# Clustered attention with transposed q and k, full float32 products and a new instruction order

## The chip, the cores and the metric

One core of a Trainium2 chip runs the whole program: TensorE (PE in the profile), VectorE (DVE), ScalarE (ACT), GpSimd (POOL) and SyncE (SP, which issues DMAs). The metric is the device time of one execution in microseconds. The kernel before takes 862.75 us, the median of three runs (862.23 to 864.58).

## What is computed

Sixteen attention heads (2 batches of 8, 768 tokens, 64 dimensions) in which a query sees only the keys of its own cluster, then a gated feed-forward layer, then a mixture of eight experts. The change lies in the attention part:

```python
q_assign = np.argmax(np.einsum('bhsd,hcd->bhsc', q_n, c_n), axis=-1)   # 16 centroids per head
k_assign = np.argmax(np.einsum('bhsd,hcd->bhsc', k_n, c_n), axis=-1)
mask = q_assign[:, :, :, None] == k_assign[:, :, None, :]
scores = np.where(mask, q @ k.T / 8, -1e9)                             # per head, 768 x 768
attn = softmax(scores)
x = attn @ v
x = _moe_ref(x, w_gate, w_val, w_out)       # sigmoid(x w_gate) * (x w_val) @ w_out
out = _moe2_ref(x, ...)                     # every token to one of 8 experts, 192 places each
```

## The kernel before, in words

**Stages.** Attention over 16 heads, 0 to 286 us; the feed-forward layer `Moe1`; its second product, the routing of tokens and the experts (`Gemm`, `Routing`, `Moe2`). `Moe1` follows attention in program order; the instructions of the rest are laid out by due times (`Streams`).

**Attention.** The class `Attention` has one method per step, and each step runs once (or once per tile) in each head. `run` sorts all steps of all heads by `ORDER[step] + n * PERIOD`, n being the head, and issues them in that sequence. Every engine works through its own instructions strictly in this order (`manual_schedule`), so `ORDER` is a hand-laid software pipeline: its keys are model times in us, and only the resulting sequence on each engine counts.

**Steps of a head.** `LD` (L109) loads q, k and v (192 KB each) with tokens on partitions. Products are made of float32r operands, each split into a part rounded to float32r and the remainder (`hi`, `lo`, L116 and L119): `Q8`, `QH`, `QL`, `KH`, `KL`, `K2`, `VH`, `VL` do so for q, k and v, mostly on GpSimd. `T_` (L157) transposes the halves of q and k on TensorE, 24 pieces of 128 columns per head (twelve for `T2`, twelve for `T1`), and `Y_` copies them from PSUM with ScalarE. `D_` (L173) multiplies them with the centroids, two times six matmuls of 256 columns; `DA`, `DD` add the two precision halves; `G1` to `G7` (L194) find the best centroid and write a one-hot code of 16 columns next to q and k, which `T1` transposes along with the low halves. `S_` (L214) makes a tile of 128 x 768 scores with four matmuls, two of which carry the code as 16 more rows, so that keys of other clusters get a huge negative score. `M_` takes the row maximum on VectorE, `E_` the exponential and row sum on ScalarE, `A_` and `C_` the reciprocal, `N_` scales P on GpSimd. `PT` (L253) transposes P in four pieces of 128 x 128 per PSUM bank, 36 pieces per head. `HI` (ScalarE, L263) and `LO` (VectorE, L267) split each transposed bank, and `AV` (L270) multiplies both with v: four matmuls of 256 columns per bank, 36 per head, the two halves of v side by side in the 128 output partitions. `OC` and `OA` add the output halves, `XH` and `XL` split the result for `Moe1`.

**PSUM.** Eight banks: three named `t` in turn (T, D, PT and others), two buffers of two banks for S, one for `av`.

**Weights.** The feed-forward weights come as float64 bits and are converted by `from64` (L369 to L384, one ScalarE and six VectorE steps). `weights(0)` and `weights(1)` convert the first two blocks of 128 columns; they are placed by a scheduler among the instructions of attention, `weights(1)` not ahead of the instructions in `LATE_W1` (L345).

## Time and profile before

| | us |
|---|---|
| median of three runs | 862.75 |
| profiled execution, its own time | 862.27 |
| its span, first to last instruction | 860.5 |
| attention, first S to last AV | 20.4 to 286.5 |
| from there to the end | 574.0 |

The profile is of one execution. A busy share counts the time in which an engine works on at least one instruction; TensorE's matmuls overlap, so their printed durations add up to more than their time, and the distance between starts is used where their pace is wanted. PE is the matmul, PEld the weight load that runs beside it. "L276" is line 276 of the kernel. The granted clock of TensorE has two levels, 1.2 and 2.4 GHz, printed as a share of the higher one.

### The profile page before, as it was taken

How to read it: one execution, taken by the hardware profiler on the slowest of the kernel's cores; microseconds unless marked ns; L12 is line 12 of the kernel's file. 1: busy time of each engine (PE TensorE's matmuls, PEld its weight loads, DVE VectorE, ACT ScalarE, POOL GpSimd, SP SyncE). 2: the span in 40 equal slices, each digit the busy share in tenths (PEclk: the TensorE clock that was granted, in tenths of full speed). 3: DMA queues.
4: the chain of work that ended last, by engine and by line, in shares of the span. 5: the costliest groups of instructions: out<-in, count | busy, mean ns of one | idle time of the engine just before them, and what ended most of it. 6: DMA issues, size and time to landing. Idle time of an engine off the chain costs nothing. (4 is left out here: it accounts for less than half of the span.)

```text
span 860.5 us, 15425 instructions
## 1 busy us (share of the span) xinstructions
PE 812.6 (94%) x5321; PEld 687.6 (80%) x5321; DVE 692.1 (80%) x1835; ACT 468.7 (54%) x993; POOL 245.7 (29%) x339
## 2 busy tenths in 40 slices
PE   3899999999999899999999999999999889889997
PEld 3799999999999687777777777887878676767886
DVE  6899999999996989998872205889988688988992
ACT  4799998998987433333321212234343534454882
POOL 4687788888865000000000000000020210211211
PEclk8999999999999999999999999999999888798999
DMA  5201101101000144453430503143261444445961
GB/s 158 81 29 37 48 29 51 35 29 56 2 1 1 57 166 145 147 185 133 141 105 1 195 1 135 50 136 102 96 208 26 123 151 131 134 143 169 309 239 37
DMA packets 51518, 86.52 MB, mean 101 GB/s; under 512 B 5592, under 2 KB 24048, under 8 KB 51440
## 3 DMA queue, kind: packets, MB, share of 16 engines
q1 hardware_dynamic: 47760, 75.53, 27.0%
q0 software_dynamic: 2048, 6.29, 2.4%
q10 hardware_dynamic: 1632, 3.72, 1.2%
q8 instruction: 42, 0.69, 0.3%
q14 instruction: 36, 0.29, 0.1%
HBM read 72.93 MB, written 12.60 MB: 99 GB/s over the span
## 5 line engine op out<-in xcount | busy, mean ns | idle before, releaser
L1095 ACT ACTIVATE w2h<-raw 128x512 fp32r<-128x512 f32 x128 | 78.8, 632 | 60.3 <-DMA raw<-in_moe_w 59.6
L267 DVE TENSOR_TENSOR ptl<-t,pth 128x512 fp32r<-128x512 f32 x144 | 94.4, 683 | 11.9 <-ACT pth L263 11.7
L229 DVE TENSOR_REDUCE sm<-s 128x1 f32<-128x768 f32 x96 | 91.2, 950 | 9.5 <-PE s L220 9.0
L117 POOL TENSOR_SCALAR P<-P,sm 128x768 f32<-128x768 f32 x96 | 86.6, 910 | 26.5 <-DVE sm L247 15.9
L657 PE MATMUL acc<-wos,yhh 128*128 128x512 f32 x288 | 91.8, 400 | 0.0
L220 PE MATMUL s<-tr 128*128 128x512 f32 (+3 forms) x384 | 90.0, 356 | 1.4 <-ACT P L234 1.2
L263 ACT ACTIVATE pth<-t 128x512 fp32r<-128x512 f32 x144 | 80.9, 600 | 14.8 <-PE t L259 12.6
L234 ACT ACTIVATE P<-s,sm 128x768 f32<-128x768 f32 x96 | 87.0, 906 | 2.1 <-DVE sm L229 2.1
L1098 DVE TENSOR_TENSOR w2l<-raw,w2h 128x512 fp32r<-128x512 f32 x128 | 84.4, 682 | 0.6 <-ACT w2h L1095 0.5
L259 PE MATMUL t<-idf,P 128*128 128x128 f32 x576 | 78.9, 273 | 0.4 <-DVE ptl L267 0.4
L1185 PE MATMUL acc<-xt,w2l 128*128 128x256 f32 x256 | 68.3, 305 | 6.8 <-DVE w2l L1098 6.8
L259 PEld LDWEIGHTS t<-idf,P 128*128 128x128 f32 x576 | 64.9, 140 | 3.0 <-POOL am L204 0.7
L220 PEld LDWEIGHTS s<-tr 80*128 80x128 f32 (+1 forms) x384 | 59.5, 192 | 6.7 <-ACT P L234 2.3
L1187 PE MATMUL acc<-xt,w2h 128*128 128x384 f32 x192 | 64.7, 360 | 0.0
L1116 POOL DMA_INDIRECT xg<-yd,idx x16 | 18.7, 1170 | 160.0 <-DVE G L915 114.4
L276 PE MATMUL av<-pth,vs 128*128 128x256 f32 x288 | 62.8, 299 | 0.8 <-DVE xf L291 0.8
L474 PE MATMUL gv<-xhi,wgh 128*128 128x512 f32 x144 | 59.5, 413 | 3.1 <-DVE h L478 3.1
L478 DVE TENSOR_TENSOR h<-gv,h 128x512 f32<-128x512 f32 x36 | 24.6, 686 | 45.8 <-ACT h L477 45.7
L657 PEld LDWEIGHTS acc<-wos,yhh 128*128 128x128 f32 x288 | 52.0, 188 | 11.3 <-issue 0.8
L477 ACT ACTIVATE h<-gv 128x512 f32<-128x512 f32 x36 | 21.2, 592 | 69.9 <-PE gv L474 68.2
L1185 PEld LDWEIGHTS acc<-xt,w2l 128*128 128x128 f32 x256 | 51.6, 205 | 9.0 <-DVE w2l L1098 8.6
L474 PE MATMUL gv<-xlo,wgh 128*128 128x512 f32 x144 | 57.7, 401 | 0.0
(227 smaller groups left out, 2084.5 us busy)
## 6 DMA issues: line engine op xcount, KB each, us to landing
raw<-in_moe_w SPq DMA_DIRECT2D x128, 256.0 KB, 3.7
...
raw<-in_q SPq DMA_DIRECT2D x16, 192.0 KB, 2.4
raw<-in_k SPq DMA_DIRECT2D x16, 192.0 KB, 2.6
raw<-in_v SPq DMA_DIRECT2D x16, 192.0 KB, 3.1
...
```

What stands on the lines that cost most here:

```text
L117: return (eng or self.nc.gpsimd).tensor_scalar(out, x, s, 1.0, op0=ALU.mult, op1=ALU.mult)
L220: self.last = self.nc.tensor.matmul(s[:, c0:c1], t[:, i, :], kk[:, c0:c1], start=(j == 0), stop=(j == 1))
L229: self.at["M", n, i] = self.nc.vector.tensor_reduce(out=self.t["sm", n, i // 2][:, 0, i % 2:i % 2 + 1], in_=self.t["s", n, i], op=ALU.max, ...
L234: self.at["E", n, i] = self.nc.scalar.activation(self.t["P", n, i // 2][:, a], self.t.pop(("s", n, i)), AF.Exp, bias=sm[:, 0, a:a + 1], ac ...
L259: self.nc.tensor.transpose(p[:, kk, a, :], P[:, a, kt * 128:(kt + 1) * 128], self.K["idf"])
L263: self.nc.scalar.activation(hi, self.t["PT", n, j, c].rearrange("p k a b -> p k (a b)"), AF.Copy)
L267: self.at["LO", n, j, c] = self.nc.vector.tensor_tensor(out=lo, in0=self.t.pop(("PT", n, j, c)).rearrange("p k a b -> p k (a b)"), in1=sel ...
L474: nc.tensor.matmul(p, w[:, d], x[:, d, cs], start=(k == 0), stop=(k == 3 * ND - 1))
L657: nc.tensor.matmul(pys[t], x[:, t], w, start=(f == 0 and k == 0), stop=(f == NF - 1 and k == 2))
L1095: nc.scalar.activation(hi, self.raw[j], AF.Copy)
L1098: nc.vector.tensor_tensor(out=lo, in0=self.raw.pop(j), in1=hi.bitcast(F32), op=ALU.subtract)
L1185: nc.tensor.matmul(p[:, 0:256], lo[:, fs], xt[d][:, 0:256], start=False, stop=False, skip_group_check=True)
```

## The change

**Inputs.** q and k are laid out transposed in memory before the launch (dimension by token, 64 x 768 per head). `LQ` loads both onto 128 partitions, q on the lower 64 and k on the upper 64; `LV` loads v apart. `T_`, `Y_`, `Q8`, `K2`, `VH`, `VL` are gone.

**Centroid products.** `D` multiplies the loaded float32 tile with a float32 centroid block: six matmuls with 128 stationary columns and 32 moving ones, each a full float32 product. `DA` and `DD` are gone. `G1` to `G5` are all on VectorE, the first two read PSUM. The one-hot code is written in bfloat16 (`nm`), `TM` transposes it (six pieces of 64 columns), and `MQ` (VectorE) and `MK` (ScalarE) write 16 rows of it, 768 columns, beside the high halves.

**Scores.** The operands are `x1q`, `x1k` (low and high halves over each other) and `x2` (high halves and code). `QH`, `KH` (GpSimd) and `QL`, `KL` (VectorE) write the halves where the operand already has the right partitions; the others are moved across partitions by DMA on SyncE's queue (`QM` one copy of 64 x 768, `KM` two), in head 0 by ScalarE copies. S keeps its four matmuls.

**Values.** `HI` copies the transposed bank as float32, `LO` is gone, and `AV` is two full float32 matmuls per bank: 64 stationary columns of v each, one on the lower and one on the upper column half of the array (`tile_position`), 256 moving columns, 18 per head. `OC` and `OA` now add the two halves of the bank's tokens. `XL` moves from GpSimd to VectorE.

**Order.** `ORDER` is new throughout, `PERIOD` is 13.30 and not 15.00. `weights(0)` is kept behind the row maximum of head 0, tile 5; the first entry of `LATE_W1` is `HI` and not `LO`. The warm-up matmul of a later stage reads the identity and no longer the centroids, with the same columns.

```diff
 def centroid_prep(tc, wk, ps, K, cen):
+
     nc = tc.nc
-    w = wk.tile([128, 4, D], F32, name="cen", tag="am")
-    c, sq, cn, ss = (w[:, i] for i in range(4))
+    K["cD"] = wk.tile([128, H, 2 * C], F32, name="cD")
+    K["idb"] = wk.tile([128, 128], BF, name="idb")
+    nc.gpsimd.memset(K["cD"], 0.0)
+    nc.gpsimd.tensor_copy(K["idb"], K["idf"])
+    for i in range(2):
+        K["nm%d" % i] = wk.tile([128, T, 64], BF, name="nm%d" % i)
+        nc.gpsimd.memset(K["nm%d" % i], 0.0)
+    w = wk.tile([128, 4, 2 * D], F32, name="cen", tag="cen")
+    c, sq, cn, ss = w[:, 0, 0:D], w[:, 1, 0:D], w[:, 2], w[:, 3]
     nc.scalar.dma_start(c, cen.rearrange("h c d -> (h c) d"))
     nc.vector.scalar_tensor_tensor(sq, c, 1.0, c, op0=ALU.mult, op1=ALU.mult, accum_out=ss[:, 0:1])
     nc.scalar.activation(ss[:, 1:2], ss[:, 0:1], AF.Sqrt)
     nc.scalar.activation(ss[:, 4:5], ss[:, 0:1], AF.Exp)
     nc.vector.tensor_scalar(ss[:, 2:3], ss[:, 1:2], 1e-6, None, op0=ALU.add)
     nc.vector.reciprocal(ss[:, 3:4], ss[:, 2:3])
-    nc.vector.tensor_scalar(cn, c, ss[:, 3:4], None, op0=ALU.mult)
-    st = wk.tile([128, 2, 2, D], F32R, name="cen_st")
-    nc.vector.tensor_copy(st[:, 0], cn[:, None, :].to_broadcast([128, 2, D]))
-    hi = st[:, 0].bitcast(F32)
-    nc.vector.tensor_tensor(out=st[:, 1], in0=cn[:, None, :].to_broadcast([128, 2, D]), in1=hi, op=ALU.subtract)
-    for s in range(2):
-        p = ps.tile([128, 512], F32R, name="t", tag="t")
-        nc.tensor.transpose(p[:, :128], st[:, s].rearrange("p a d -> p (a d)"), K["idr"])
-        pv = p[:, :128].bitcast(F32).rearrange("p (h c) -> p h c", h=H)
-        nc.scalar.activation(K["cT"][:, 0:8, s, :], pv, AF.Copy)
-        nc.scalar.activation(K["cT"][:, 8:15, s, :], pv[:, 0:7], AF.Copy)
+    nc.vector.tensor_scalar(cn.rearrange("p (a d) -> p a d", a=2), c[:, None, :].to_broadcast([128, 2, D]), ss[:, 3:4], None, op0=ALU.mult)
+    p = ps.tile([128, 512], F32, name="t", tag="t")
+    nc.tensor.transpose(p[:, :128], cn, K["idf"])
+    for i in range(2):
+        nc.scalar.activation(K["cD"][64 * i:64 * i + 64, :, C * i:C * i + C],
+                             p[64 * i:64 * i + 64, :128].rearrange("p (h c) -> p h c", h=H), AF.Copy)
...
+    "LQ": -46.189, "D": -31.541, "G1": -28.524, "KH": -28.300, "G2": -28.154, "LV": -27.355, "KL": -21.005,
+    "G3": -20.706, "QH": -20.568, "KM": -18.540, "QM": -17.387, "G4": -15.187, "G5": -14.169, "TM": -14.045,
+    "MK": -12.434, "QL": -12.097, "MQ": -11.726, "S1": -8.463, "S0": -8.159, "M1": -4.144, "M0": -3.661, "E1": -2.907,
+    "S2": -2.231, "E0": -1.148, "S3": -0.896, "A1": -0.854, "M2": -0.409, "C1": 0.122, "N0": 0.523, "E2": 0.713,
+    "N1": 0.829, "M3": 1.113, "S4": 1.282, "E3": 1.346, "PT01": 1.444, "A3": 1.689, "C3": 1.699, "HI01": 2.054,
+    "PT00": 2.104, "PT02": 2.907, "HI00": 3.025, "M4": 3.185, "N3": 3.204, "HI02": 3.762, "E4": 3.851, "S5": 3.991,
+    "M5": 4.047, "AV00": 4.127, "AV01": 4.193, "E5": 4.243, "A5": 4.356, "N2": 4.591, "AV02": 4.618, "C5": 4.781,
+    "PT10": 4.818, "OC0": 4.838, "HI10": 4.839, "PT11": 5.427, "PT12": 7.185, "HI11": 7.794, "HI12": 8.653,
+    "OA0": 8.696, "N5": 8.857, "AV10": 9.211, "AV11": 9.667, "AV12": 9.675, "N4": 10.029, "PT20": 10.475,
+    "PT21": 11.172, "OC1": 11.601, "OA1": 11.910, "HI20": 12.226, "PT22": 12.269, "AV20": 12.578, "HI21": 13.085,
+    "AV21": 13.256, "HI22": 13.813, "AV22": 14.225, "OC2": 15.185, "OA2": 16.481, "XH": 21.654, "XL": 25.279,
 }
-PERIOD = 15.00
+PERIOD = 13.30
...
+    def x1(self, n, w):
+        return self.new(("x1" + w, n), [128, S], F32R, "x1" + w, 3)
+
+    def x2(self, n):
+        return self.new(("x2", n), [128, 2, S], F32R, "x2", 3)
+
+    def LQ(self, n):
+        b, h = divmod(n, H)
+        r = self.t["raw", n] = self.ld.tile([128, S], F32, name="raw", bufs=3)
+        for i, src in enumerate((self.q, self.k)):
+            self.nc.sync.dma_start(r[64 * i:64 * i + 64], src[b, h])
+
+    def LV(self, n):
+        b, h = divmod(n, H)
+        r = self.t["v", n] = self.ld.tile([128, T, D], F32, name="rawv", bufs=4)
+        self.nc.sync.dma_start(r, self.v[b, h].rearrange("(p t) d -> p t d", t=T))
 
     def QH(self, n):
-        nq = self.new(("nq", n), [128, T, 128 + C], F32R, "nq", 2)
-        self.hi(nq[:, :, 64:128], self.t["q8", n], 1.0, self.first(n))
+        self.hi(self.x2(n)[0:64, 0], self.t["raw", n][0:64], 0.125, self.nc.vector if n == 0 else None)
+
+    def KH(self, n):
+        self.hi(self.x2(n)[64:128, 1], self.t["raw", n][64:128])
+
+    def move(self, n, out, x):
+
+        if n == 0:
+            self.nc.scalar.activation(out, x.bitcast(F32), AF.Copy)
+        else:
+            self.nc.sync.dma_start(out.bitcast(F32), x.bitcast(F32))
+
+    def QM(self, n):
+        self.move(n, self.x1(n, "q")[64:128], self.x2(n)[0:64, 0])
+
+    def KM(self, n):
+        x = self.x2(n)
+        self.move(n, self.x1(n, "k")[0:64], x[64:128, 1])
+        self.move(n, x[0:64, 1], x[64:128, 1])
...
+    def QL(self, n):
+        self.nc.vector.scalar_tensor_tensor(self.x1(n, "q")[0:64], self.t["raw", n][0:64], 0.125, self.x2(n)[0:64, 0].bitcast(F32),
+                                            op0=ALU.mult, op1=ALU.subtract)
...
+        self.nc.vector.tensor_tensor(out=self.x1(n, "k")[64:128], in0=self.t["raw", n][64:128],
+                                     in1=self.x2(n)[64:128, 1].bitcast(F32), op=ALU.subtract)
+    def D_(self, n):
+        p = self.bank(("D", n), [128, 512])
         for t in range(T):
-            self.nc.tensor.matmul(p[:, 32 * t:32 * t + 256], self.t["tr", n, 2][:, i * T + t, :], w, start=True, stop=True)
-
-    def dots(self, n, i, s):
-        return self.t["D", n, i][:, 0:32 * T].rearrange("p (t s c) -> p t s c", s=2, c=C)[:, :, s]
-
-    def DA(self, n, i):
-        if ("am", n) not in self.t:
-            self.new(("am", n), [128, 4, 2 * T, C], F32, "am", 1)
-            self.new(("amx", n), [128, 2, 2 * T], F32, "amx", 2)
-        self.nc.scalar.activation(self.t["am", n][:, 1, i * T:(i + 1) * T], self.dots(n, i, 1), AF.Copy)
-
-    def DD(self, n, i):
-        am = self.t["am", n]
-        s = slice(i * T, (i + 1) * T)
-        self.nc.vector.tensor_tensor(out=am[:, 0, s], in0=self.dots(n, i, 0), in1=am[:, 1, s], op=ALU.add)
+            self.nc.tensor.matmul(p[:, 32 * t:32 * t + 32], self.t["raw", n][:, t * 128:(t + 1) * 128], self.K["cD"][:, n % H],
+                                  start=True, stop=True)
...
+    def TM(self, n):
+
+        p = self.bank(("TM", n), [128, 1024], BF)
+        for t in range(T):
+            self.nc.tensor.transpose(p[0:64, t * 128:(t + 1) * 128], self.K["nm%d" % (n % 2)][:, t], self.K["idb"])
+
+    def MQ(self, n):
+        self.nc.vector.tensor_scalar(self.x2(n)[64:64 + C, 0], self.t["TM", n][0:C, 0:S], -1.0, 1.0, op0=ALU.mult, op1=ALU.add)
+
+    def MK(self, n):
+        self.nc.scalar.activation(self.x2(n)[64:64 + C, 1], self.t["TM", n][32:32 + C, 0:S], AF.Copy, scale=-BIG)
...
+        x = self.x2(n)[0:D + C]
+        for j, (t, kk) in enumerate(((self.x1(n, "q"), self.x1(n, "k")), (x[:, 0], x[:, 1]))):
             for c0, c1 in ((0, 512), (512, S)):
-                self.last = self.nc.tensor.matmul(s[:, c0:c1], t[:, i, :], kk[:, c0:c1], start=(j == 0), stop=(j == 1))
+                self.last = self.nc.tensor.matmul(s[:, c0:c1], t[:, i * 128:(i + 1) * 128], kk[:, c0:c1], start=(j == 0), stop=(j == 1))
...
-        hi = self.new(("hi", n, j, c), [128, 2, 256], F32R, "pth", 4)
-        self.nc.scalar.activation(hi, self.t["PT", n, j, c].rearrange("p k a b -> p k (a b)"), AF.Copy)
-
-    def LO(self, n, j, c):
-        lo = self.new(("lo", n, j, c), [128, 2, 256], F32R, "ptl", 4)
-        self.at["LO", n, j, c] = self.nc.vector.tensor_tensor(out=lo, in0=self.t.pop(("PT", n, j, c)).rearrange("p k a b -> p k (a b)"),
-                                     in1=self.t["hi", n, j, c].bitcast(F32), op=ALU.subtract)
+        x = self.new(("hi", n, j, c), [128, 2, 256], F32, "pt", 6)
+        self.at["HI", n, j, c] = self.nc.scalar.activation(x, self.t.pop(("PT", n, j, c)).rearrange("p k a b -> p k (a b)"), AF.Copy)
 
     def AV(self, n, j, c):
+
         if c == 0:
             self.t["av", n, j] = self.ps.tile([128, 256], F32, name="av", bufs=1)
-        av = self.t["av", n, j]
-        for s, x in enumerate((self.t.pop(("hi", n, j, c)), self.t.pop(("lo", n, j, c)))):
-            for kk in range(2):
-                self.nc.tensor.matmul(av, self.t["vs", n][:, 2 * c + kk, :], x[:, kk, :],
-                                      start=(c == 0 and s == 0 and kk == 0), stop=(c == 2 and s == 1 and kk == 1))
+        av, x = self.t["av", n, j], self.t.pop(("hi", n, j, c))
+        for kk in range(2):
+            self.nc.tensor.matmul(av[64 * kk:64 * kk + 64], self.t["v", n][:, 2 * c + kk], x[:, kk], start=(c == 0), stop=(c == 2),
+                                  tile_position=(0, 64 * kk))
...
-            self.lo(x[2], x[0], x[1])
+            self.nc.vector.tensor_tensor(out=x[2], in0=x[0], in1=x[1].bitcast(F32), op=ALU.subtract)
...
-LATE_W1 = ("LO", B * H - 1, 2, 2), ("E", B * H - 1, 5), ("N", B * H - 1, 5)
+LATE_W1 = ("HI", B * H - 1, 2, 2), ("E", B * H - 1, 5), ("N", B * H - 1, 5)
...
-                m1.weights(0)
+                with ExitStack() as late:
+                    late.enter_context(tc.issue_after(at.at["M", 0, 5].ins))
+                    m1.weights(0)
...
+        if name in ("q", "k"):
+            a = np.ascontiguousarray(a.reshape(B, H, 128, T, D).transpose(0, 1, 4, 3, 2)).reshape(B, H, D, S)
```

## Rows read from the trace of the kernel before

**Rows 1.** Busy time by stretch: us, engines with instructions, clock, DMA.

```profile
60.00:243.20 183.20, 182.88 (x1530) 175.63 (x1529) 169.69 (x428) 168.85 (x373) 149.30 (x206) 1.00 0.11 34
255.20:286.50 31.30, 30.45 (x217) 27.90 (x216) 22.60 (x53) 21.13 (x43) 15.76 (x24) 1.00 0.01 1
286.50:860.50 574.00, 544.00 (x3174) 434.06 (x3173) 439.89 (x1206) 225.58 (x464) 36.98 (x44) 0.96 0.40 130
```

**Rows 2.** Line 204, 60 to 243 us: ns min/median/max, first and last start.

```profile
L204 POOL TENSOR_TENSOR am<-am,desc x11: 591/596/600, 70.5 to 228.9; 128x192 f32<-128x192 f32 x11
```

**Rows 3.** Timeline of TensorE in mid-attention: start us, us, instruction, count.

```profile
155.68 0.52 PE L164 MATMUL t<-idr,nk 128*80 128x128 f32 x6
156.04 0.62 PE L259 MATMUL t<-idf,P 128*128 128x128 f32 x4
156.42 0.95 PE L220 MATMUL s<-tr 128*128 128x512 f32 x4
157.21 1.04 PE L259 MATMUL t<-idf,P 128*128 128x128 f32 x8
...
162.39 1.59 PE L178 MATMUL t<-cT,tr 128*128 128x256 f32 x12
163.82 0.40 PE L276 MATMUL av<-pth,vs 128*128 128x256 f32 x2
164.06 0.40 PE L276 MATMUL av<-ptl,vs 128*128 128x256 f32 x2
```

**Rows 4.** Timeline of TensorE around the last logit matmuls, behind attention.

```profile
519.11 0.39 PE L657 MATMUL acc<-wos,yhl 128*128 128x512 f32 x1
519.42 0.64 PE L462 MATMUL pl<-h,wps 128*32 128x512 f32 x4
...
519.88 0.61 PE L462 MATMUL pl<-h,wps 128*32 128x512 f32 x4
...
520.42 0.73 PE L657 MATMUL acc<-wos,yhh 128*128 128x512 f32 x2
520.99 0.39 PE L657 MATMUL acc<-wos,yhl 128*128 128x512 f32 x1
```

**Rows 5.** Timeline of TensorE at line 455, float32 matmuls with few columns.

```profile
334.00 0.95 PE L455 MATMUL wg<-g2r,wT 128*128 128x8 f32 x8
334.81 0.48 PE L474 MATMUL gv<-xlo,wgh 128*128 128x512 f32 x1
```

**Rows 6.** Groups by line, 60 to 243 us: busy us, mean ns, idle before.

```profile
L267 DVE TENSOR_TENSOR ptl<-t,pth 128x512 fp32r<-128x512 f32 x104 | 68.3, 683 | 5.7 <-ACT pth L263 5.5
L229 DVE TENSOR_REDUCE sm<-s 128x1 f32<-128x768 f32 x70 | 66.5, 950 | 6.8 <-PE s L220 6.5
L170 ACT ACTIVATE tr<-t 128x512 fp32r<-128x512 f32 x36 | 20.4, 602 | 0.3
```

**Rows 7.** Timeline of the start: first head, and the weight conversion (L379 and on).

```profile
6.53 0.26 ACT L62 ACTIVATE cT<-t 128x112 fp32r<-128x112 f32 x1
8.78 1.88 PE L178 MATMUL t<-cT,tr 128*128 128x256 f32 x8
...
10.68 0.43 DVE L379 SCALAR_TENSOR_TENSOR ff<-fp,raw 128x256 f32<-128x256 f32 x1 [3.53 <-ACT fp L378]
...
18.88 1.22 DVE L379 SCALAR_TENSOR_TENSOR ff<-fp,raw 128x256 f32<-128x256 f32 x1
20.42 1.61 PE L220 MATMUL s<-tr 128*128 128x512 f32 x4
...
24.52 0.95 DVE L229 TENSOR_REDUCE sm<-s 128x1 f32<-128x768 f32 x1
```

**Rows 8.** Timeline: first row maximum of head 15, last matmuls of attention.

```profile
255.19 0.94 DVE L229 TENSOR_REDUCE sm<-s 128x1 f32<-128x768 f32 x1
...
286.19 0.40 PE L276 MATMUL av<-ptl,vs 128*128 128x256 f32 x2
```

**Rows 9.** DMA issues on the page: instruction, count, KB each, us to landing.

```profile
raw<-in_v SPq DMA_DIRECT2D x16, 192.0 KB, 3.1
```

More of the change, by code (lines that the diff above doesn't have):

```diff
@@ L99, in new @@
     def new(self, key, shape, dt, name, bufs):
-        x = self.wk.tile(shape, dt, name=name, bufs=bufs)
-        self.t[key] = x
-        return x
+        if key not in self.t:
+            self.t[key] = self.wk.tile(shape, dt, name=name, bufs=bufs)
+        return self.t[key]
     def bank(self, key, shape, dt=F32):
@@ L152, in VL @@
-    def VL(self, n):
-        o = D * (n % 2)
-        vs = self.t["vs", n]
-        self.lo(vs[:, :, D - o:2 * D - o], self.t["raw", n][:, 2], vs[:, :, o:o + D])
-    def T_(self, n, w, c):
-        p = self.bank(("T", n, w, c), [128, 512], F32R)
-        for j in range(4):
-            i, t = divmod(4 * c + j, T)
-            o = ((0, 0) if w == 2 else (64, 128))[i]
-            r = self.ROWS[w]
-            src = self.t["nk" if i else "nq", n][:, t, o:o + r]
-            self.nc.tensor.transpose(p[0:r, j * 128:(j + 1) * 128], src, self.K["idr"])
@@ L1147, in warm @@
             yield "P", 0.2
-            self.nc.tensor.matmul(p, self.K["idr"], self.K["cT"].rearrange("p a s c -> p (a s c)"), start=True, stop=True)
+            self.nc.tensor.matmul(p, self.K["idr"], self.K["idr"][:, None, 0:32].to_broadcast([128, 15, 32]), start=True, stop=True)
     def high(self, k, d, px, xt):
```

105 lines of the change are left out of this document (21 added, 84 removed), and 15 rows, old and new, of the table ORDER.

## Prediction

> **What bounds the kernel now.** I read the busy table by stretch first. From 60 to 243 us, in the middle of attention, TensorE is busy 182.88 of 183.20 us at full granted clock, VectorE 169.69, ScalarE 168.85, GpSimd 149.30 [rows 1]. So TensorE sets the pace there, with two engines 7% behind it. The stage that follows attention is the longest stretch, 574 us from 286.5 us to the end [rows 1], and the change doesn't touch its work. What is to be won lies before 286.5 us.
>
> One instruction that occurs once in a head gives the period: eleven of them from 70.5 to 228.9 us, so 158.4/10 = 15.84 us per head [rows 2]. Next I read TensorE's instructions in order of time [rows 3], always from the start of one group to the start of the next, because a matmul's printed duration (0.27 to 0.48 us) holds a drain that the next one overlaps. A tile of scores S (four matmuls) takes 157.21 - 156.42 = 0.79 us; four transposes of P take 0.38, so 0.10 each; six transposes of the narrow parts of q and k take 0.36, so 0.06; twelve centroid matmuls D take 1.43; two matmuls of AV take 0.24 [rows 3]. Per head: S 6 x 0.79 = 4.7, P 36 x 0.10 = 3.6, T at least 24 x 0.06 = 1.4, D 1.4, AV 36 x 0.12 = 4.3. The sum is 15.4 of 15.84; the wide half of T and small waits share the 0.4 that is left.
>
> Then the two ends of the stage. The first row maximum M starts at 24.5 us [rows 7], the first one of head 15 at 255.2, and the last AV matmul at 286.2 [rows 8]. At the start the chain is load, split, transposes, D, argmax, transposes again, S, with VectorE's weight conversion (L379 and on) pushed between its links [rows 7].
>
> **The change part by part, TensorE's work per head.**
>
> *T goes* (24 transposes): -1.4 to -1.8, the latter if all of the 0.4 is its own; I take -1.6. *TM comes*: six bfloat16 transposes of 64 columns. No row has them; the narrow ones of [rows 3] give 6 x 0.06 = 0.4, and as a bound 6 x 0.10 = 0.6.
>
> *D* becomes six full float32 matmuls. A float32 product shows as two weight loads and two matmuls: the four of one call of `prime` (L455) leave eight records. With few columns to stream they go at the pace of the load: eight in 334.81 - 334.00 = 0.81 us, 0.10 each [rows 5]. So 12 x 0.11 = 1.3 against 1.4.
>
> *AV* becomes 18 full float32 matmuls of 64 output partitions, in pairs on the two column halves of the array. The nearest rows are the logit matmuls, four float32 products of 512 columns on four column quarters [rows 4]. The four first records start together at 519.42, the four second ones at 519.88: the quarters run at the same time, and a pass of 512 columns takes 0.46 us, where a plain matmul of that width takes half of it (two from 520.42 to 520.99 with one extra cost inside). A pass of 256 columns is thus 0.23, and a pair of AV matmuls two passes, 0.46; nine pairs 4.1. Going into column tiles and out again costs extra: the last plain matmul starts at 519.11 and the tiles at 519.42, 0.31 where 0.23 is usual, so 0.08; the second pass holds until 520.42, 0.54 instead of 0.46, so 0.08; and the two matmuls behind take 0.57 instead of 0.46, so 0.11. In all 0.27. In the new order the AV come three in a row (AV00 to AV02 behind S5, AV10 to AV12 behind D, AV20 to AV22 behind TM), so three such switches per head, 0.8. AV: 4.1 + 0.8 = 4.9 against 4.3, so +0.6. Bounds: 4.2 if a pass is pure streaming (0.21) and the exit is hidden, and rival 3's value if the halves don't overlap.
>
> Sum per head: -1.6 + 0.4 - 0.1 + 0.6 = -0.7, and -0.9 with T at its upper value. Waits of the old T and D for their copies go as well, so I take the latter: **15.84 - 0.9 = 14.9 us**, with 14.1 (AV 4.2, T 1.8) to 15.5 as bounds.
>
> *The other engines* must stay under that. VectorE: 14.7 per head now (169.69/183.20 x 15.84). It loses nine LO of 0.683 [rows 6], 6.1. It gains KL and QL, 768 columns each; L379 takes 0.43 for 256 [rows 7], so 1.3 each at most; MQ, at most the 0.95 of M, which has 768 columns as well [rows 6]; XL (384 columns, 0.65) and G3 (192, 0.3) from GpSimd. About 13.2. One thing can stretch that: L379 takes 1.22 in place of 0.43 at 18.9 us [rows 7], while GpSimd runs a two-input subtract; those all leave GpSimd, but its scalings N, QH, KH stay. I allow 13 to 14. ScalarE: 14.6 less six Y of 0.6 [rows 6], plus MK (768 columns, as M's 0.95): 12. GpSimd: it loses eleven preparatory steps for QH and KH at N's size. So TensorE stays the bound, with VectorE 1 to 2 us behind.
>
> *The halves by DMA* (QM, KM) add three SBUF copies of 192 KB per head to SyncE, behind whose waits LQ and LV queue. A load of that size lands in 3.1 us [rows 9]. KM stands ten units of the order ahead of S1, QM nine; LQ runs a full three heads ahead. I cost it at nothing; the slack covers it. If the cover is gone, each head waits 2 to 3 us.
>
> **The start.** The centroid copies end at 6.8 us now [rows 7]; the new chain leaves out the split into two halves and one transpose, say 6.0. D of head 0 at the low clock, taken from L178's eight in 1.88 us (0.21 each) [rows 7]: 12 x 0.21 = 2.5, to 8.5. Then VectorE in its new order: G1, G2, KL, G3, QH, G1 of head 1, G4, G2 of head 1, G5. Seven steps G over 192 columns at no more than 192/256 of L379's 0.43 make 2.3, KL and QH (768 columns) 0.8 to 1.3 each, 2: to 12.8. QL and MQ 2 (TM runs beside QL), to 14.8; S at the low clock 1.6 (L220 at 20.42 [rows 7]), so the first M at some **16**, where it was 24.5: -8.5 (bounds 12.5, if the G steps take half of that and the clock is up, and 20, if two-input steps stretch as L379 did). Part of this comes from weights(0), whose conversion now may not start ahead of M of tile 5 in head 0. Its work (two matrices in two halves of six VectorE steps, 24 at no more than 0.43: 10 us) moves behind that, where VectorE has 1 to 2 us free per head: it costs 0 to 10, and I take 3.
>
> **From the first M to that of head 15.** Now 255.2 - 24.5 = 230.7, 6.9 less than 15 x 15.84, because the first heads run without their predecessors' AV. New: 15 x 14.9 = 223.5; the pipeline is shallower (S to AV22 spans 22.4 units of 13.3 instead of 36.9 of 15), so the same gain is about 3, which weights(0) takes back. 223.5: -7.2.
>
> **The tail.** Now 286.5 - 255.2 = 31.3 [rows 1]. New, behind M1 of head 15: five tiles S 3.9; of head 14 twenty transposes 2.2 and two AV groups of (3 x 0.46 + 0.27 = 1.65) 3.3; of head 15 P 3.9 and AV 4.95. Sum 18.3, and 2 of waits in the draining pipeline (ScalarE's copies and the single av bank). 20.3: -11 (bounds 8 and 14).
>
> **Sum.** End of attention at 16 + 223.5 + 20.3 = 259.8 us instead of 286.5, -26.7. The profiled execution took 862.27 us (span 860.5 and 1.8 around it), the median is 862.75. 862.3 - 26.7 = 835.6, by the median **836 us**. The later stages move forward as they are; what the planner may reorder at the seam, I cost at +-2.
>
> **Rivals.**
>
> 1. *The period doesn't fall.* VectorE's 13.2 grows through GpSimd's port, or the new in-order sequence makes TensorE wait for av's single bank (AV10 needs OA0 behind VectorE's queue). For: VectorE would be at 89% and ScalarE at 81%. Against: both were at 92% before, and TensorE lost almost nothing. Then 15 x 15.8 between the same ends: 16 + 237 + 21 = 274, so 850.
> 2. *A block at the start.* SyncE waits for weight buffers: fetches of weights(1) need what weights(0) frees later than before, and KM, QM, LQ of heads 1 and 2 queue behind them. Once 5 to 10 us: 841 to 846.
> 3. *Slower: the column halves don't run at the same time.* Place: the nine AV pairs. Price: four passes per pair instead of two, 9 x 0.92 + 0.8 = 9.1 for 4.9, so 19.1 per head. 15 x 19.1 = 286, tail 27, end at 329: 905. It loses as soon as AV costs over 6.7 per head, which is where 26.7 us are used up (1.8 x 15). Against: the four quarters of [rows 4] started together. For: those were quarters, with one product each, and here the same half is used three times running, so that a weight load must fit behind a running pass. The page TensorE: Matmul & The Clock Gate of the Trainium skill (Part 3, The mechanism) states that a weight load overlaps running matmuls only when the row group differs, and the two column halves share all rows. By that rule the loads of all 36 passes stand bare. In rows: at the 0.10 of [rows 5] per load that is 3.6 more, 18.5 per head, some 895, and I count it in this rival. [rows 4] speak against it: the second pass of the quarters starts 0.46 us behind the first, hardly more than two plain matmuls, with no room for four bare loads.
> 4. *A better one:* AV at 4.2 and T at its upper value: 14.1 per head, 824; with a first M at 12.5, 820.
>
> **How the numbers follow.** Forecast as worked out (with rival 4 as its lower edge) 0.70: 820 to 848 with the bounds of start, period and tail not all at one side. Rival 1: 0.15. Rival 2: 0.08. Rival 3: 0.07. The range 818 to 854 takes in all but rival 3 and a tenth of the others. What measurement can tell from no change is about 0.3%, 2.6 us. Faster by more 0.91, within 0.02, slower 0.07.
>
> **What would show it.** In the new profile: the period of any once-a-head instruction (14.9), the first M (16), last AV (260), records of one AV group (three pairs, 1.65 from first start to what follows), VectorE's busy share in the middle (85 to 92%), and the stretch behind attention unchanged near 574. It is wrong if AV pairs take over 0.7 us, if TensorE shows gaps in mid-attention, or if the last stretch changes by more than 3 us.

## The result and the profile after

The changed kernel takes 840.24 us (median), the kernel before 862.49 in the same comparison: a ratio of 0.974, interval 0.970 to 0.979. The prediction was 836.0 in a range of 818 to 854. One of the change's four executions took 2848.47 us, in a slow state, and the ratio is of the other three. The profiled execution took 839.76 us, its span is 838.0.

The same three stretches as in [rows 1], busy time of each engine: mid-attention, from the first row maximum of head 15 to the last AV, and the rest.

```profile
60.00:240.00 180.00, 176.74 (x1360) 139.77 (x1359) 158.85 (x288) 150.90 (x302) 103.30 (x108) 1.00 0.30 75
244.80:270.20 25.40, 25.40 (x170) 18.66 (x168) 12.38 (x25) 17.27 (x35) 8.71 (x16) 1.00 0.01 2
270.20:838.00 567.80, 539.23 (x3177) 431.72 (x3173) 436.67 (x1202) 226.12 (x464) 37.34 (x44) 0.97 0.40 131
```

TensorE (first busy figure) is still the bound, 176.74 of 180.00 us, VectorE (third) 88%. The next lines answer to [rows 2], [rows 7] and [rows 8]: G3, once a head; the first row maximum of head 0 and of head 15; TensorE's last AV.

```profile
L169 DVE TENSOR_TENSOR am<-am,desc x12: 966/966/972, 66.6 to 230.8; 128x192 f32<-128x192 f32 x12
15.64 0.95 DVE L198 TENSOR_REDUCE sm<-s 128x1 f32<-128x768 f32 x1
244.84 0.94 DVE L198 TENSOR_REDUCE sm<-s 128x1 f32<-128x768 f32 x1
269.74 0.82 PE L238 MATMUL av<-pt,rawv 128*64 128x256 f32 x6
```

Twelve G3 from 66.6 to 230.8 make 164.2/11 = 14.93 us per head, where it was 15.84. The last AV record starts at 270.18. TensorE's order in mid-attention, to be set beside [rows 3]:

```profile
142.51 0.83 PE L155 MATMUL t<-cD,raw 128*128 128x32 f32 x6
143.28 1.51 PE L238 MATMUL av<-pt,rawv 128*64 128x256 f32 x12
144.72 0.66 PE L226 MATMUL t<-idf,P 128*128 128x128 f32 x4
145.13 0.59 PE L194 MATMUL s<-x1k,x1q 128*128 128x512 f32 x2
145.56 0.52 PE L194 MATMUL s<-x 80*128 80x512 f32 x2
145.92 1.04 PE L226 MATMUL t<-idf,P 128*128 128x128 f32 x8
146.71 0.60 PE L194 MATMUL s<-x1k,x1q 128*128 128x512 f32 x2
...
150.15 0.27 PE L226 MATMUL t<-idf,P 128*128 128x128 f32 x1
150.64 1.42 PE L226 MATMUL t<-idf,P 128*128 128x128 f32 x11 [0.22 <-POOL P L104]
```

Three AV pairs, twelve records, take 144.72 - 143.28 = 1.44 us. The sum, term by term, in the profiled execution:

| us | predicted | measured |
|---|---|---|
| first M | 16.0 | 15.6 |
| first M to head 3 | 3 x 14.9 = 44.7 | 52.2 |
| head 3 to head 14 | 11 x 14.9 = 163.9 | 164.4 |
| head 14 to head 15 | 14.9 | 12.6 |
| tail to the last AV | 20.3 | 25.3 |
| end of attention | 259.8 | 270.2 |
| from there to the end | 574.0 | 567.8 |

So attention ends 10.4 us later than predicted, and 6.2 come back behind it. As differences to the kernel before: start -8.9 us (predicted -8.5), first M to that of head 15 -1.5 (-7.2), tail -6.0 (-11), behind attention -6.2 (0 +-2). The shorter period is nearly used up by the slow first intervals: the first three intervals between heads are 17.3, 19.7 and 15.2 us; these stretches show why.

```profile
15.60:33.00 17.40, 17.39 (x92) 14.55 (x91) 13.13 (x28) 10.51 (x20) 7.25 (x7) 1.00 0.45 110
33.00:52.60 19.60, 15.75 (x119) 12.04 (x118) 19.44 (x42) 13.89 (x28) 11.69 (x9) 1.00 0.33 87
52.60:67.80 15.20, 14.30 (x107) 10.89 (x108) 13.70 (x26) 12.59 (x26) 9.02 (x10) 1.00 0.43 114
```

In the first, TensorE is busy throughout; in the second it stands still for 3.85 us and VectorE is full, 19.44 of 19.60. Two causes, then: TensorE's own pace, and VectorE with weights(0) in it. The pace is seen in TensorE's order of time:

```profile
20.39 0.84 PE L194 MATMUL s<-x1k,x1q 128*128 128x512 f32 x2
21.03 0.84 PE L194 MATMUL s<-x 80*128 80x512 f32 x2
30.10 0.51 PE L194 MATMUL s<-x 80*128 80x512 f32 x2
30.45 0.51 PE L194 MATMUL s<-x1k,x1q 128*128 128x512 f32 x2
30.80 0.52 PE L194 MATMUL s<-x 80*128 80x512 f32 x2
```

Two matmuls of S take 0.64 us at 20 us and 0.35 at 30; the change of pace comes at some 27 us. The trace's records of the granted clock begin there, at 27.16 us, at the upper level.

### The profile page after: what moved, and what is told of

Its sections match the earlier page's. It is cut to its first block, busy times and chain, and to the rows that moved or that the text cites. A ratio compares the mean times of both kernels' runs of the same rounds, so it can differ in the third digit from the quotient of the medians.

```text
span 838.0 us, 14521 instructions
## 1 busy us (share of the span) xinstructions
PE 795.3 (95%) x5032; PEld 633.3 (76%) x5032; DVE 659.3 (79%) x1622; ACT 436.8 (52%) x882; POOL 178.9 (21%) x202
## 5 line engine op out<-in xcount | busy, mean ns | idle before, releaser
L104 POOL TENSOR_SCALAR P<-P,sm 128x768 f32<-128x768 f32 x96 | 104.7, 1101 | 109.2 <-DVE sm L214 91.3
L198 DVE TENSOR_REDUCE sm<-s 128x1 f32<-128x768 f32 x96 | 89.4, 948 | 6.8 <-PE s L194 6.1
L226 PE MATMUL t<-idf,P 128*128 128x128 f32 x576 | 82.6, 280 | 5.6 <-POOL P L104 4.1
L230 ACT ACTIVATE pt<-t 128x512 f32<-128x512 f32 x144 | 78.4, 596 | 18.1 <-PE t L226 16.6
L226 PEld LDWEIGHTS t<-idf,P 128*128 128x128 f32 x576 | 64.9, 142 | 24.5 <-POOL P L104 9.2
L238 PE MATMUL av<-pt,rawv 128*64 128x256 f32 x576 | 73.7, 386 | 1.6 <-DVE xf L253 0.8
L194 PE MATMUL s<-x1k,x1q 128*128 128x512 f32 x192 | 58.3, 386 | 0.1
L423 PE MATMUL gv<-xhi,wvl 128*128 128x512 f32 x144 | 57.2, 397 | 0.0
L423 PE MATMUL gv<-xhi,wvh 128*128 128x512 f32 x144 | 57.1, 397 | 0.0
L423 PE MATMUL gv<-xhi,wgl 128*128 128x512 f32 x144 | 57.1, 397 | 0.0
```

What stands on the lines that cost most here:

```text
L104: return (eng or self.nc.gpsimd).tensor_scalar(out, x, s, 1.0, op0=ALU.mult, op1=ALU.mult)
L198: self.at["M", n, i] = self.nc.vector.tensor_reduce(out=sm[:, 0, i % 2:i % 2 + 1], in_=self.t["s", n, i], op=ALU.max, axis=AX.X, negate=True)
L226: self.nc.tensor.transpose(p[:, kk, a, :], P[:, a, kt * 128:(kt + 1) * 128], self.K["idf"])
L230: self.at["HI", n, j, c] = self.nc.scalar.activation(x, self.t.pop(("PT", n, j, c)).rearrange("p k a b -> p k (a b)"), AF.Copy)
L238: self.nc.tensor.matmul(av[64 * kk:64 * kk + 64], self.t["v", n][:, 2 * c + kk], x[:, kk], start=(c == 0), stop=(c == 2), tile_position=(0 ...
L423: nc.tensor.matmul(p, w[:, d], x[:, d, cs], start=(k == 0), stop=(k == 3 * ND - 1))
```

## The experiments

The marks below come from each run's profiled execution. "Steady" is the mean interval between heads 10 and 14 (weights(0) is through by then in all of them), "experts" the time from the first to the last matmul of the experts' first product. e2, e4, e7, e8 and e10 have one execution each.

| kernel | first M | intervals 1, 2, 3 | steady | last AV | experts | time (median, or one run) |
|---|---|---|---|---|---|---|
| before | 24.5 | 10.7, 14.2, 15.8 | 15.8 | 286.3 | 199.9 | 862.49 |
| the change | 15.6 | 17.3, 19.7, 15.2 | 14.9 | 270.2 | 196.1 | 840.24 |
| e1_nohold | 19.5 | 18.3, 15.1, 14.3 | 14.9 | 269.8 | 197.7 | 840.55 |
| e2_w0skip | 17.9 | 17.0, 15.1, 14.3 | 14.9 | 266.6 | 198.8 | 839.14 |
| e3_warm | 15.5 | 16.2, 19.7, 15.3 | 14.9 | 269.0 | 197.7 | 843.25 |
| e4_wide | 15.7 | 17.7, 18.9, 16.8 | 17.9 | 311.9 | 198.3 | 884.96 |
| e5_late0 | 15.6 | 17.3, 15.1, 14.3 | 14.9 | 271.9 | 198.5 | 845.24 |
| e6_late0_warm | 15.4 | 17.0, 15.2, 14.3 | 14.9 | 273.0 | 198.6 | 843.75 |
| e7_actmove | 15.6 | 17.8, 18.6, 15.3 | 16.1 | 284.5 | 201.4 | 859.15 |
| e8_halfs | 15.6 | 16.1, 20.0, 15.9 | 14.4 | 262.1 | 198.5 | 834.27 |
| e9_spread | 16.5 | 16.6, 15.1, 14.8 | 14.9 | 269.7 | 201.0 | 839.98 |
| e10_heat | 16.0 | 16.4, 19.7, 15.2 | 14.9 | 269.7 | 197.0 | 840.01 |
| e11_spread_heat | 16.7 | 15.0, 15.1, 14.8 | 14.9 | 268.4 | 197.6 | 838.40 |

This product, which none of the edits touches, takes 196 to 201 us. Effects of a few us within attention are therefore read from the last AV, not from the whole time. The start has some scatter too: in e9, e10 and e11 VectorE's first step on the centroids starts at 3.34, 3.22 and 3.06 us instead of 2.49, because their load lands later, and the first M carries part of that.

**e1_nohold: weights(0) may start at once.**

```diff
-                with ExitStack() as late:
-                    late.enter_context(tc.issue_after(at.at["M", 0, 5].ins))
-                    m1.weights(0)
+                m1.weights(0)
```

> The new kernel without the hold on weights(0), as the kernel before had it. Theory A (the conversion's 10 us of VectorE work decide the start): they move in front of the first row maximum, first M from 15.6 to 19 or 20 us, the two long head intervals behind it from 17.3 and 19.7 to 13 to 15, end of attention within 3 us of 270. Theory B (TensorE's half-speed matmuls up to 27 us decide it): first M later as above, but the interval from head 0 to 1 stays over 16 us, end of attention 4 us or more later. Time 838 to 841 by A, 844 to 847 by B.

The first M comes 3.9 us later, intervals 2 and 3 are 5.4 us shorter, and the last AV stands 0.4 us earlier. The hold moves the price of weights(0) from ahead of the first M to behind it and saves next to nothing. Each theory has one half: the end is where A has it, but interval 1 is 18.3 and not 13 to 15, as B has it.

**e2_w0skip: weights(0)'s VectorE steps left out** (the kernel leaves out the conversion of the first weight block, of which there are two matrices in two halves each; one ScalarE copy stands in for six VectorE steps).

```diff
-                from64(tc, cw, raw[:, d], [128, ND // n, 128], w[:, d], g)
+                if ft == 0:
+                    nc.scalar.activation(w[:, d], raw[:, d, :, 1].bitcast(F32), AF.Copy)
+                else:
+                    from64(tc, cw, raw[:, d], [128, ND // n, 128], w[:, d], g)
```

> The new kernel with the six VectorE steps per half matrix of weights(0) left out (the float64 conversion of the first block is replaced by one ScalarE copy, so the feed-forward values of that block are others). Theory A: the interval of heads 1 to 2 falls from 19.7 to 15, that of heads 0 to 1 by 1 to 2 at most (its first half lies ahead of the conversion), end of attention 5 to 7 us earlier. Theory B: 2 us earlier at most. Theory C (SyncE's queue blocked by weight fetches): the fetch of the next block goes out earlier as well, KM and QM of head 3 with it, same 5 us, but VectorE would show idle time between 35 and 55 us.

Intervals 2 and 3 sum to 29.4 us instead of 34.9: the conversion costs 5.5 there. The last AV gains only 3.6, since the first M comes 2.3 us later here: ScalarE's stand-in copies are in the way of head 0's own, and TensorE waits 2.5 us for x1q. Of the 3.6 us, 0.7 are left at the end of the span, because the expert stage took 198.8 us this time instead of 196.1.

**e3_warm: nine extra matmuls from 1.85 to 6 us**, so that TensorE has worked ahead of head 0's D.

```diff
+    heat = ps.tile([128, 512], F32, name="t", tag="t")
+    for _ in range(5):
+        nc.tensor.matmul(heat[:, 0:480], K["idr"], K["idr"][:, None, 0:32].to_broadcast([128, 15, 32]), start=True, stop=True)
...
+    for _ in range(4):
+        nc.tensor.matmul(heat[:, 0:480], K["idr"], K["idr"][:, None, 0:32].to_broadcast([128, 15, 32]), start=True, stop=True)
```

> The new kernel with nine more matmuls of 480 columns on TensorE between 1.8 and 6 us, before the first centroid matmuls. Theory B: the clock is up when D of head 0 starts, twelve records of D take 1.35 and not 2.5 us, first M at 14, the interval of heads 0 to 1 falls from 17.3 to 13, and part of that comes back in the next one; end of attention 3 to 6 us earlier, 835 to 837. Theory A alone: the heads end where they did, since VectorE's conversion sets the second interval: at most 1 us. If the clock doesn't rise on nine matmuls: no change.

The full pace returns at 22.5 us instead of 27, interval 1 falls by 1.1, and the last AV comes 1.2 earlier: what 4.5 us less of half pace are worth. That is far less than theory B's 3 to 6. The whole time did not fall.

**e4_wide: AV without column halves** (each product takes 128 stationary columns, so the outputs are not the attention's values; the work of TensorE is what it would be with no pairing).

```diff
-            self.nc.tensor.matmul(av[64 * kk:64 * kk + 64], self.t["v", n][:, 2 * c + kk], x[:, kk], start=(c == 0), stop=(c == 2),
-                                  tile_position=(0, 64 * kk))
+            self.nc.tensor.matmul(av, self.t["v", n][:, 2 * c:2 * c + 2].rearrange("p t d -> p (t d)"), x[:, kk],
+                                  start=(c == 0 and kk == 0), stop=(c == 2 and kk == 1))
```

> The new kernel with AV as float32 products of 128 stationary columns over the whole width of the array instead of pairs on the two column halves (the two 64-column blocks of v go together, so the values summed are others; same number of instructions). It shows what running the halves at the same time is worth. By the prediction's third rival a bank then costs four passes of 0.23 us, AV 8.4 per head in place of 4.3, period 14.9 to 18.9, time 840 + 60 = 900. If it is under 880, AV was not on TensorE's critical path to that extent.

Each of the 36 passes now occupies the whole array. Twelve records from TensorE's order of time:

```profile
153.81 2.75 PE L238 MATMUL av<-pt,rawv 128*128 128x256 f32 x12
156.40 0.60 PE L226 MATMUL t<-idf,P 128*128 128x128 f32 x4
```

2.59 us instead of 1.44; AV takes 7.8 us a head instead of 4.3, of which 0.5 come back because the transposes no longer wait for P. The period is 17.9, and the kernel takes 884.96 us, slower than before the change. So the two halves do run at the same time, and the sign of the whole change hangs on it. Its price without pairing is 3.0 us a head, not the 4.2 of rival 3: a pass costs 2.59/12 = 0.216, where the prediction had 0.23 with the switch on top.

**e5_late0: weights(0) held behind head 4.**

```diff
-                    late.enter_context(tc.issue_after(at.at["M", 0, 5].ins))
+                    late.enter_context(tc.issue_after(at.at["M", 4, 5].ins))
```

> The conversion of weights(0) may not start ahead of the last row maximum of head 4 (tile 5), where the change has head 0; nothing else differs, and all of the work is still done. Theory A (VectorE is full in the first two heads, and has 1.7 us per head to spare afterwards): the first M stays at 15.6 us, the first intervals fall from 17.3 and 19.7 to at most 17.0 and 15.1, as without the conversion, one or two intervals behind head 4 grow by at most 1 us in all, and the last AV comes at 266.5 to 268 us instead of 270.2. Rival (the conversion costs the same wherever it stands, since in an in-order queue each of its steps delays a row maximum): the intervals of heads 5 to 7 take up the 3.5 us, and the last AV stays at 270. Theory C (the fetches of the next weights, which wait for the buffers of weights(0), block SyncE's queue): it gets worse, since more heads' loads stand behind them; last AV at 272 or later. Whole kernel: 837 by A, 840 by the rival.

The rival holds, and more. Intervals 2 and 3 shrink as in e2, but those of heads 4 to 6 become 15.5, 20.2 and 16.0, 6.9 us above three steady ones, and the last AV is 1.7 us later. The stretches of these three intervals, and the costliest wait of the middle one (who waits for whom; us in all, times, the longest):

```profile
77.50:93.00 15.50, 15.24 (x120) 12.20 (x119) 14.88 (x30) 12.61 (x26) 8.91 (x10) 1.00 0.32 78
93.00:113.20 20.20, 15.69 (x116) 11.77 (x115) 20.06 (x43) 13.90 (x28) 12.26 (x10) 1.00 0.31 85
113.20:129.20 16.00, 15.54 (x107) 11.72 (x108) 14.38 (x27) 12.47 (x26) 8.76 (x10) 0.89 0.42 108
```

```profile
POOL P L104 <- DVE sm L214: 7.9, 2, 5.6
```

VectorE is full for one head. The reciprocal C (L214) stands behind conversion steps, GpSimd waits up to 5.6 us for it before it can scale P, the transposes wait for P, and TensorE loses the time. The same line in the change itself, from 33 to 52.6 us:

```profile
POOL P L104 <- DVE sm L214: 7.8, 3, 5.1
```

Not all of the 6.9 us is VectorE's. In the third stretch the granted clock is 0.89, and TensorE begins it at half pace, after it has waited in the second one (busy 15.69 of 20.20):

```profile
113.25 2.76 PE L238 MATMUL av<-pt,rawv 128*64 128x256 f32 x12 [0.95 <-DVE xf L253]
115.94 1.05 PE L226 MATMUL t<-idf,P 128*128 128x128 f32 x4
```

Three AV pairs take 2.69 us here and four transposes 0.77, against 1.44 and 0.41 in the change: up to 1.6 of the 6.9. Theory C (SyncE's queue) has nearly the same end, 272, but no engine's wait from 77 to 129 us was ended by a DMA.

**e6_late0_warm: e5 and e3 together.**

> The later weights(0) and the nine extra matmuls ahead of head 0's D together. If conversion (3.5 us) and half pace (1.2 us) are separate causes, both gains add: last AV at 265.4 us (270.2 - 3.5 - 1.2). If they hide one another, it stays at that of the later weights(0) alone, 266.6. The whole kernel follows the last AV to within the 2 to 3 us by which the expert stage differs from run to run in the earlier experiments: 835 to 838 us.

The last AV is 273.0, later than with either edit. Half pace lasts until 27 us here although the nine matmuls are there, so the gain of e3 is not had, and whether the two add is not tested. The end is later than e5's because intervals 7 and 8 are 17.1 and 15.6 instead of 16.0 and 15.2; the granted clock is 0.90 from 113 to 130 us.

**e7_actmove: all halves moved by ScalarE, no DMA** (undoes one part of the change).

```diff
-        if n == 0:
+        if n >= 0:
```

> The halves QM and KM are moved by three ScalarE copies in every head and not in head 0 alone; SyncE's queue loses 45 DMAs. ScalarE has 12.5 us per head now; three copies of 64 x 768 at the 0.90 of the exponentials (768 columns too) add 2.7 and make 15.2, over TensorE's 14.93. Theory (the DMA is what keeps ScalarE below the bound): period 15.2 to 15.8, last AV 275 to 283 us, kernel 845 to 853. Rival (ScalarE would absorb it, or the DMAs delay something themselves): period unchanged at 14.9 and the kernel at 840 or below.

Worse than the theory: period 16.1, last AV 14.3 us later, 859.15 us. Mid-attention and its costliest waits:

```profile
60.00:240.00 180.00, 169.89 (x1272) 130.17 (x1271) 144.88 (x269) 165.85 (x314) 100.40 (x102) 1.00 0.13 35
```

```profile
POOL P L104 <- ACT pt L230: 27.6, 5, 5.5
DVE xf L253 <- ACT xf L249: 17.3, 11, 1.8
PEld s L194 <- ACT P L203: 9.7, 11, 0.9
```

ScalarE is at 92% (165.85 of 180), not at 100: what it does late, copies of PT and of av, other engines wait for in their order. The 45 DMAs that replace these copies thus carry most of the change's gain, and cost nothing that shows.

**e8_halfs: one of the two products of S left out**, to see what lies below TensorE.

```diff
-        for j, (t, kk) in enumerate(((self.x1(n, "q"), self.x1(n, "k")), (x[:, 0], x[:, 1]))):
+        for j, (t, kk) in ((1, (x[:, 0], x[:, 1])),):
...
-                self.last = self.nc.tensor.matmul(s[:, c0:c1], t[:, i * 128:(i + 1) * 128], kk[:, c0:c1], start=(j == 0), stop=(j == 1))
+                self.last = self.nc.tensor.matmul(s[:, c0:c1], t[:, i * 128:(i + 1) * 128], kk[:, c0:c1], start=True, stop=True)
```

> Leaves out one of the two products of every score tile (the one with the low halves), two of the four matmuls of S: TensorE has 6 x 0.40 = 2.4 us less per head, 12.5. It asks what the next bound is. Theory (VectorE is next, with 158.85 of 180.00 us in mid-attention, 13.2 per head): period 13.2 to 13.6, last AV at some 245 to 250 us, VectorE at 97% or more in mid-attention. Rival (the in-order sequence or ScalarE with 12.5 per head stretches it): period 13.8 to 14.5 with no engine above 95%. If TensorE were not the bound at all, the period would stay at 14.9.

The rival holds: the period falls by 0.54 us only, to 14.39, with no engine above 92%.

```profile
60.00:225.00 165.00, 151.66 (x1163) 113.38 (x1163) 146.74 (x275) 142.10 (x289) 103.28 (x106) 1.00 0.33 81
```

```profile
PEld t L226 <- POOL P L104: 13.9, 13, 1.2
PE t L226 <- POOL P L104: 10.5, 12, 0.9
```

TensorE waits in each head for GpSimd's scaling of P. By these waits the next bound is not an engine but the chain S, M, E, C, N, PT in its fixed order, half a us below TensorE's sum. This fits what e5 showed: VectorE's idle 12% don't take in weights(0).

**e9_spread: weights(0) in four pieces behind heads 2, 4, 6 and 8.**

```diff
-                from64(tc, cw, raw[:, d], [128, ND // n, 128], w[:, d], g)
+                with ExitStack() as late:
+                    if ft == 0:
+                        late.enter_context(tc.issue_after(self.hold.pop(0)))
+                    from64(tc, cw, raw[:, d], [128, ND // n, 128], w[:, d], g)
...
+                    m1.hold = [at.at["M", h, 5].ins for h in (2, 4, 6, 8)]
```

> The four half matrices of weights(0) may not start ahead of the last row maximum of heads 2, 4, 6 and 8, one each, where the change allows all four behind head 0. The runs so far: held behind head 0, the conversion makes the intervals of two heads 17.3 and 19.7 long; held in one piece behind head 4, those of three (15.5, 20.2, 16.0). Theory (in one piece VectorE gets 10 us of extra work within 20, where it has 1.7 us to spare per head; the row sums' reciprocals, and with them GpSimd and the transposes, wait behind it): four pieces of 2.6 to 3.3 us, two heads apart, find 3.4 us of slack each, so no interval exceeds 16 us and the last AV comes at 266.5 to 268 us (270.2 in the change, 271.9 with the one piece behind head 4). Rival (each step costs its own time wherever it stands, since all engines work in order and the next chain lies only 0.5 us per head below TensorE, as the run with half of S showed): four times 1.5 to 2 us are lost, last AV at 272 to 275. Whole kernel: 837 to 841 by the theory, 843 to 847 by the rival.

Neither. Seven of the eight intervals from head 2 to head 10 are longer than the steady 14.93, at most 16.1; from head 2 (48.2 us) to head 10 (172.1) it takes 123.9 us where eight steady ones take 119.4. The conversion costs 4.5 us spread out, 5.5 in one piece behind head 0 and 6.9 behind head 4, at least 5.3 of them apart from the half pace there. Two stretches of 15 us that follow one another, the first with a piece, the second nearly without:

```profile
60.00:75.00 15.00, 13.98 (x110) 10.99 (x108) 14.38 (x28) 11.88 (x25) 8.62 (x8) 1.00 0.29 74
75.00:90.00 15.00, 14.84 (x118) 11.72 (x114) 13.47 (x25) 12.57 (x26) 9.05 (x11) 1.00 0.32 82
```

VectorE is at 96% in the first, and TensorE loses 1 us. Only about half of the conversion's 10.1 us of VectorE steps is hidden, wherever it stands.

**e10_heat: sixteen more extra matmuls, at 9.0 and 12.3 us**, in TensorE's waits around TM of head 0 (on top of e3's nine; a method `heat` writes them into the bank of av).

```diff
...
-                    at.run(also=[(-1.7, lambda: m1.fetch(0))])
+                    at.run(also=[(-1.7, lambda: m1.fetch(0)), (-14.1 / PERIOD, lambda: at.heat(12)), (-14.0 / PERIOD, lambda: at.heat(4))])
```

> Beside the nine extra matmuls ahead of head 0's D, twelve more of 480 columns stand between D of head 1 and the code transposes TM of head 0, and four behind TM, into the bank of av that nothing uses yet: they fill the 2.7 and 1.0 us in which TensorE waits for VectorE there. weights(0) stays as in the change. In the run with nine, TensorE went back to half pace at TM and kept it until 22.5 us. Theory B (half pace in 11 to 27 us is what makes the first interval 17.3 instead of under 14.9): S of head 0 at full pace from 12 us on, first M at 15 to 16, first interval 13 to 15, and the last AV 2 to 4 us earlier, 266 to 268. Rival (VectorE's chain of head 1 and the conversion set the second interval anyway): the first interval falls, the second grows by as much, and the last AV stays at 269 to 270.

The first S go at full pace, and then it drops again:

```profile
13.26 0.51 PE L206 MATMUL s<-x1k,x1q 128*128 128x512 f32 x2
18.06 1.01 PE L206 MATMUL s<-x1k,x1q 128*128 128x512 f32 x2
18.86 0.84 PE L206 MATMUL s<-x 80*128 80x512 f32 x2
```

```profile
15.00:20.00 5.00, 4.90 (x24) 4.34 (x25) 4.29 (x10) 1.88 (x4) 0.00 (x0) 0.67 0.79 181
20.00:25.00 5.00, 4.98 (x22) 3.76 (x21) 4.65 (x8) 3.25 (x6) 3.18 (x3) 0.50 0.16 43
```

The granted clock (third figure from the end) is 0.67 and then 0.50, the lower level, although TensorE has been busy for 4.9 and 4.98 of 5 us; it fell after TensorE had waited 1.1 us for VectorE's MQ at 13.8 to 14.9 us. Interval 1 loses 0.9, the first M comes 0.4 later, and the last AV 0.5 earlier. Theory B is not tested by this, since half pace was back (granted clock 0.50 from 16.8 to 26.9 us).

**e11_spread_heat: e9 and e10 together.**

> Both edits together: weights(0) in four pieces behind heads 2, 4, 6 and 8, and TensorE kept working from 2 to 12 us. If half pace and the conversion are the two causes of the late start and each goes away, the last AV comes at 263 to 265 us: 270.2 less 3 for the conversion and 3 for the pace. If the filling of the pipeline is set by VectorE's chain in heads 0 and 1, it stays at that of the four pieces alone. The whole kernel, with 2 to 3 us of difference from run to run in the expert stage: 832 to 838 by the first, 837 to 841 by the second.

Last AV 268.4, 1.8 us before the change and 1.3 before e9; interval 1 is 15.0. That lies between the two expectations, and half pace had not gone: the granted clock is 0.50 again from 19.3 to 26.1 us. The ratio to the kernel before is 0.971 (0.968 to 0.975), to be set beside 0.974 (0.970 to 0.979) of the change: lower, but the intervals overlap, so that it beats the change is not shown.

## Why the prediction held, and where its steps failed

The forecast was the likeliest case and it came: faster, by a shorter period and a shorter start. That 836.0 lies only 4.2 us from 840.24 is in part luck: attention ends 10.4 us late, and 6.2 come back in a stretch that the prediction left as it was. Two of its three signs of being wrong came as well: the last stretch changed by more than 3 us, and TensorE has gaps in mid-attention, 3.26 of 180 us; an AV pair over 0.7 us did not (0.48). Point by point:

- **TensorE's sum per head, 14.9, measured 14.93.** By distances between starts over ten heads (83.0 to 232.3 us): S 4.85, PT 4.17, AV 4.33, D 1.3 to 1.4, TM 0.31, against 4.7, 3.6, 4.9, 1.3 and 0.4. Two errors cancel. AV is cheaper: a group of three pairs takes 1.44 and not 1.65, and leaving the halves costs next to nothing behind it (144.72 to 145.13, 0.41 for four transposes, 0.38 in [rows 3]). PT is dearer: about once a head a transpose waits for GpSimd's P, 0.4 us with what follows (150.15 to 150.64 above). The old kernel's starts over ten heads (81.1 to 239.5 us) give S 4.55, PT 3.49, AV 4.71, T 1.67 and D 1.43. So the old AV was read too low, at 4.3 from two matmuls: AV falls by 0.4 where the prediction let it grow by 0.6, while PT and S grow by 0.7 and 0.3, which it had at nothing.
- **AV pairs.** [rows 4] were the right rows: 0.24 per pass of two halves, and e4 shows 0.216 for one pass that has the array to itself. The rule on page TensorE: Matmul & The Clock Gate of the Trainium skill (Part 3, The mechanism), that weight loads overlap only across row groups, would have left the loads of 36 passes bare; the trace disagrees, 1.44 us for twelve records with their loads.
- **The other engines.** VectorE 158.85/180.00 x 14.93 = 13.2, as predicted; ScalarE 12.5 instead of 12.
- **The halves by DMA at nothing**: held; no engine's wait from 15 to 240 us was ended by a DMA. What the prediction did not see is what they are worth: e7 puts 14.3 us on the end of attention.
- **The start.** The first M at 16 was right (15.6); of the 8.9 us gained, 3.9 come from the hold of weights(0) (e1). The next step failed: "the same gain of about 3, which weights(0) takes back". Conversion: 5.5 (e2, e5), not 3. It was sized by the idle time that VectorE has on average, when the order is fixed and the chain that runs through VectorE has only half a us per head to spare below TensorE's sum (e8). Fill: a loss of 2.0 and not a gain of 3 (e5, whose first three intervals hold no conversion: 17.3 + 15.1 + 14.3 = 46.7 against 44.7). The old kernel had its half pace ahead of its first M at 24.5 us (granted clock 0.50, line below); the new one has its first M at 15.6 us with half pace until 27, and the prediction charged that to D and one S only. e3 gives back 1.1 of it, and e11 2.3 of interval 1 for a first M 1.1 later. Together 5.5 + 2.0 = 7.5, which is 52.2 - 44.7. That half pace makes the 2.0 is argued from e3 and e11; no run was without it.

```profile
13.80:23.90 10.10, 5.70 (x31) 5.01 (x32) 9.51 (x21) 3.37 (x7) 8.17 (x10) 0.50 0.17 52
```

- **The tail.** Predicted 20.3, measured 25.3, with errors of both signs; the gain of 6.0 lies outside the stated 8 to 14. TensorE's starts in that stretch: 34 matmuls of `Moe1` stand among the last AV, 8.5 us, which the sum left out (they stood there in the old kernel too, within its 31.3). Against that no waits (2 allowed: TensorE is busy 25.40 of 25.40) and AV at 7.1 instead of 8.2. The interval before it is 2.3 shorter than a steady one, since no further head is prepared in it (D alone is 1.3).
- **The seam, +-2 allowed, -6.2 measured.** 4.1 of it lie in `Moe1`: from the last AV to its last matmul 229.0 us before, 224.9 in the change, and the same 224.9 in e1, e2 and e3, whatever the last AV. First before, then after, TensorE's order of time:

```profile
292.95 0.50 PE L474 MATMUL gv<-xhi,wgh 128*128 128x512 f32 x1 [3.05 <-DVE h L478]
293.84 0.63 PE L474 MATMUL gv<-xhi,wgh 128*128 128x512 f32 x1
294.27 0.63 PE L474 MATMUL gv<-xlo,wgh 128*128 128x512 f32 x1
```

```profile
272.08 0.51 PE L423 MATMUL gv<-xlo,wgh 128*128 128x512 f32 x1 [1.53 <-DVE xlo L273]
276.62 0.50 PE L423 MATMUL gv<-xhi,wgh 128*128 128x512 f32 x1 [1.01 <-DVE h L427]
```

Before, one wait of 3.05 us was followed by matmuls 0.43 apart instead of 0.23, at the lower level:

```profile
293.60:297.00 3.40, 3.40 (x10) 2.62 (x9) 3.39 (x7) 1.01 (x2) 0.00 (x0) 0.50 0.13 19
```

After, two waits of 1.53 and 1.01 are not followed by such matmuls. By distances between starts, waits and slow matmuls together make 2.2 of the 4.1; the other 1.9 is the router's product (`pl`, 64 records), which holds TensorE for 10.9 us in eleven pieces, before for 12.8 in thirteen. Of the remaining 2.1 us, the experts' first product gives 3.8, within its scatter, and 1.6 are lost between the two.
- **Rivals.** 1: no, the period fell; 3: no, e4 shows its mechanism and that its sign would have been right. 2 (SyncE): the early loss is there, 7.5 us, but VectorE's and TensorE's: no engine's wait from 15 to 68 us was ended by a DMA, and e7, without the copies in SyncE's queue, has 51.7 us in the first three intervals, against 52.2. 4: AV came near its lower value (4.33 against 4.2), but PT and S took it back.

What stays open: why the experts' first product takes between 196 and 201 us in kernels that are alike there. The going of T (1.67 us per head by the old trace) and the new order were not tried apart from the rest; their share is argued from the sum.
